# Cosine attention on one core: head 0's queries in natural order, one rsqrt chain for two heads, and the QK wave as two tasks

## The chip, the cores and the metric

The kernel runs on one core of a Trainium2 chip. The metric is the device time of one execution in microseconds (us). Runs are repeated; medians are quoted. A ratio is the mean time of one kernel's fast runs over the mean of the other's fast runs of the same rounds on the same chip, with a 95% interval, so it is not quite the ratio of the medians that are quoted.

Engine names in the profile: PE is TensorE (matmul), PEld its weight load, DVE is VectorE, ACT is ScalarE, POOL is GpSimd, SP is SyncE, which here only issues DMAs. An entry such as "SPq" or "ACTq" is such an engine issuing a DMA.

## The reference

Thirty-two heads, 2048 queries and keys each, head size 20, bfloat16. Queries and keys are normalised, the logits get one factor per head, and a softmax over the keys follows.

```python
B, H, S, D = 1, 32, 2048, 640;  Dh = D // H          # Dh = 20
def reference(q, k, v, t):
    eps = 1e-6
    qn = q / (jnp.sqrt((q * q).sum(axis=-1, keepdims=True)) + eps)
    kn = k / (jnp.sqrt((k * k).sum(axis=-1, keepdims=True)) + eps)
    logits = jnp.einsum('bhqd,bhkd->bhqk', qn, kn) * t[None, :, None, None]
    attn = _softmax(logits, axis=-1)
    return jnp.einsum('bhqk,bhkd->bhqd', attn, v)
```

## The kernel before

The program is a list of tasks. A task has an engine, a duration, its dependences and a priority. A list scheduler runs the tasks in model time and so fixes, once and for all, the order of the instructions on each engine. On the chip each engine takes its instructions in this order, and waits where a dependence isn't met (in e1 below one such wait holds VectorE for 2.5 us, with ready work behind it). **So the modelled durations and the priorities are part of the program: they decide its order.**

```python
def add(self, eng, name, fn, dur, deps=(), pri=0.0, lat=0.0, dma=None): ...

def schedule(self):                      # list scheduling in model time
    ...
    _, _, t = heapq.heappop(ready[e])    # of what is ready, the lowest pri first
    t.start = now
    t.end = now + t.dur
    if e == "PE":
        kind = t.name[:2]
        if kind != last_pe[0]:
            t.end += 0.09                # modelled cost of a change of kind, qk or pv
    ...
    order[e].append(t)
```

The exponentials of the logits are shared between two engines. A unit is 128 keys by 512 queries. Most units go to ScalarE in **waves** of three: TensorE computes QK for three units into one of two PSUM slots, ScalarE takes one exponential of 128x1536 from PSUM into a ring of 36 units in SBUF, and TensorE later multiplies four units of the ring with V (PV). The rest goes to VectorE in **tiles** of four units, which get an approximate exponential by integer arithmetic: four evictions of 128x512 from the single PSUM bank `psD`, then three operations on 128x2048 integers and one multiplication. A tile gives TensorE four QK matmuls and three PV groups. A head has 16 rows of four units; 3 or 4 of the rows are VectorE tiles.

```python
DVE_TILES = [4 if h % 3 == 1 else 3 for h in range(H)]          # 107 tiles in all
...
def add_wave(w):
    us = waves[w]; slot = w % 2
    def f_qk(eng, tk):      # first two units that use different halves of the PE rows
        pair = next(((i, i + 1) for i in range(len(us) - 1)
                     if A_units[us[i]][2] // 2 != A_units[us[i + 1]][2] // 2), ())
        for i in list(pair) + [i for i in range(len(us)) if i not in pair]:
            h, r, g = A_units[us[i]]
            last = qk_mm(eng, h, r, g, psA[...], 32 if w < WPLAIN else 64 if i in pair else 128)
        return last
    deps = [act.get(w - 2)] + ...
    qk = add("PE", f"qkA{w}", f_qk, 0.24 if w < WPLAIN else 0.55 if len(us) > 1 else 0.24,
             deps, due_a(us[0]) - 100)
    ...
    act[w] = add("ACT", f"exp{w}", ..., 0.065 + n / 1200.0, [qk] + war, 0)
```

In front of this stands the **preparation** of a head: load, square, sum, an inverse square root by a bit trick and two Newton steps (eight small operations that depend on each other), normalise, transpose by DMA, rotate the keys by DMA.

```python
def add_prep(h):
    due = h - 2.2                          # priority of this head's preparation
    for nh in range(4):                    # queries, permuted: four strided loads
        src = bass.AP(q.tensor, q[0, h].offset + nh * D, [[16 * D, 32], [4 * D, 4], [512 * D, 4], [1, D]])
        ...                                # ldq on SP (two of head 0's on ACT)
    ...                                    # ldk, ldv on SP; ldv waits only for its buffer
    dv("sq", ...128x640..., 0.86); dv("sum", ..., 0.86)
    dv("rs", ...128x32..., 0.12)           # eight of these, one after the other
    norm[h] = dv("norm", ...128x640..., 0.86)
    trn[h] = ...; rot[h] = ...             # DMA transpose, rotated copies
```

Of the kernel before, what the change touches and what calls it, by code (L numbers as in the profile page):

```python
# [12 lines left out]
I32 = mybir.dt.int32  # L13
# [26 lines left out]
class Program:  # L40
# [75 lines left out]
    def plan_waits(self, sem_of):  # L116
# [55 lines left out]
def bass_standalone__qk_norm__prompt_kernel(  # L172
# [13 lines left out]
    NB = 4  # L186
    NT = 3
    NX = 3
    DVE_TILES = [4 if h % 3 == 1 else 3 for h in range(H)]
    WPLAIN = 5  # L190
    PE_GROUP = 0.23
    SH_ENG, SH_DUR = "DVE", 0.60

    with ExitStack() as es:  # L194
# [6 lines left out]
        vaug = [sbuf(f"vaug{i}", [128, R, 32], BF16) for i in range(NB)]  # L201
        sq = sbuf("sq", [128, 2 * R, D], F32)
        rs = {x: sbuf(f"rs_{x}", [128, 2 * R], F32) for x in ("sum", "u", "a", "b", "y", "r")}
        qkn = [sbuf(f"qkn{i}", [128, 2 * R, 32], BF16) for i in range(2)]
# [5 lines left out]
        xt = [sbuf(f"xt{i}", [128, 2048], I16) for i in range(NX)]  # L210
        ee = [sbuf(f"ee{i}", [128, 2048], I16) for i in range(NX)]
        ss = [sbuf(f"ss{i}", [128, 2048], I16) for i in range(NX)]
        mm = [sbuf(f"mm{i}", [128, 2048], I16) for i in range(2)]
        tt = [sbuf(f"tt{i}", [128, 2048], FP16) for i in range(NX)]
# [10 lines left out]


        def memset(ap, val):
            return lambda eng, tk: eng.memset(ap, val)

        ld_t = add("SP", "ld_t", lambda eng, tk: eng.dma_start(  # L230
            tb16[:, :], bass.AP(t.tensor, 0, [[0, 128], [1, H]])), 0.06, lat=2.5, dma="t", pri=-50)
        scr0 = add("DVE", "scr0", memset(act_scr[:, :], 0.0), 0.1, pri=-100)
        warm = add("ACT", "warm", lambda eng, tk: eng.activation(
            act_scr[:, :], act_scr[:, :], ACT.Exp), 1.5, [scr0], pri=-100)
        z_qkn = [add("POOL", "z", memset(qkn[i][:, :, D:32], 0.0), 0.5, pri=-90 + i) for i in range(2)]
        z_qz = [add("DVE" if i else "POOL", "z", memset(qz[i][:, :, :], 0.0), 1.8, pri=-85 + i) for i in range(NT)]
        z_kx = add("POOL", "z", memset(kx[:, :], 0.0), 0.9, pri=-95)
        z_v = []
        for i in range(NB):
            a = add("POOL", "z", memset(vaug[i][:, :, D + 1:32], 0.0), 0.3, pri=-80 + i)  # L240
            b = add("POOL", "z", memset(vaug[i][:, :, D:D + 1], 1.0), 0.2, pri=-80 + i)
            z_v.append([a, b])
        tcp = add("DVE", "tcp", lambda eng, tk: eng.tensor_copy(t_f32[:, :], tb16[:, :]), 0.1, [ld_t], pri=-1)
# [3 lines left out]
        for h in range(H):  # L247
            nd = DVE_TILES[h]
            for r in range(R - nd):

                A_units += [(h, (g + r) % 4 if h == 0 and r < 4 else r, g) for g in range(NG)]
            D_tiles += [(h, r) for r in range(R - nd, R)]
        NA = len(A_units)
        nA_head = [(R - DVE_TILES[h]) * NG for h in range(H)]
        a0 = [sum(nA_head[:h]) for h in range(H + 1)]
        waves = [list(range(i, min(i + WAVE, NA))) for i in range(0, NA, WAVE)]

# [5 lines left out]
        ld_v, norm, trn, rot = {}, {}, {}, {}  # L263
        qk_users = {h: [] for h in range(H)}
        pv_users = {h: [] for h in range(H)}

# [3 lines left out]
        prep_deps = []  # L270
        qz0 = []

        def add_prep(h):
            b, b2, bt = h % NB, h % 2, h % NT
            due = h - 2.2
            war = ([norm[h - NB]] if h >= NB else []) + ([trn[h - 2]] if h >= 2 else [])
            lds = []
            for nh in range(4):
                src = bass.AP(q.tensor, q[0, h].offset + nh * D,
                              [[16 * D, 32], [4 * D, 4], [512 * D, 4], [1, D]])  # L280
                dst = qk_sb[b][32 * nh:32 * nh + 32, 0:R, :].rearrange("p (c g) d -> p c g d", g=4)
                lds.append(add("ACT" if h == 0 and nh >= 2 else "SP", f"ldq{h}", lambda eng, tk, dst=dst, src=src: eng.dma_start(dst, src),  # L282
                               0.6, war, due - 0.5 + 0.01 * (nh >= 2), lat=2.5, dma=f"q{b}a" if h == 0 and nh >= 2 else f"q{b}"))
            src_k = k[0, h].rearrange("(p r) d -> p r d", p=128)
            lds.append(add("SP", f"ldk{h}", lambda eng, tk: eng.dma_start(qk_sb[b][:, R:2 * R, :], src_k),
                           0.6, war, due - 0.51, lat=2.5, dma=f"k{b}"))
            src_v = v[0, h].rearrange("(p r) d -> p r d", p=128)
            warv = pv_users[h - NB] if h >= NB else z_v[b]
            ld_v[h] = add("SP", f"ldv{h}", lambda eng, tk: eng.dma_start(vaug[b][:, :, 0:D], src_v),
                          0.6, warv, due - 0.4, lat=3.0, dma=f"v{b}")  # L290

            def dv(name, fn, dur, deps):
                return add("DVE", name + str(h), fn, dur, deps, due)
            x = qk_sb[b]
            c = [dv("sq", lambda eng, tk: eng.tensor_tensor(sq[:, :, :], x[:, :, :], x[:, :, :], ALU.mult),  # L295
                    0.86, lds + prep_deps)]
            c.append(dv("sum", lambda eng, tk: eng.tensor_reduce(rs["sum"][:, :], sq[:, :, :], AXIS_X, ALU.add),  # L297
                        0.86, [c[-1]]))
            c.append(dv("rs", lambda eng, tk: eng.tensor_scalar(
                rs["u"][:, :].bitcast(I32), rs["sum"][:, :].bitcast(I32), -0.5, 1597463007.0, ALU.mult, ALU.add),  # L300
                0.12, [c[-1]]))
            cur = rs["u"]
            for tgt in (rs["y"], rs["r"]):
                c.append(dv("rs", lambda eng, tk, cur=cur: eng.tensor_tensor(  # L304
                    rs["a"][:, :], cur[:, :], cur[:, :], ALU.mult), 0.12, [c[-1]]))
                c.append(dv("rs", lambda eng, tk: eng.scalar_tensor_tensor(  # L306
                    rs["b"][:, :], rs["a"][:, :], -0.5, rs["sum"][:, :], ALU.mult, ALU.mult), 0.12, [c[-1]]))
                c.append(dv("rs", lambda eng, tk, cur=cur, tgt=tgt: eng.scalar_tensor_tensor(
                    tgt[:, :], rs["b"][:, :], 1.5, cur[:, :], ALU.add, ALU.mult), 0.12, [c[-1]]))
                cur = tgt  # L310
            c.append(dv("rs", lambda eng, tk: eng.tensor_scalar(
                rs["r"][:, 0:R], rs["r"][:, 0:R], t_f32[:, h:h + 1], None, ALU.mult), 0.12, [c[-1], tcp]))
            if h == 0:
                first_head(x, c[-1])
                return
            war = [trn[h - 2]] if h >= 2 else [z_qkn[b2]]
            norm[h] = dv("norm", lambda eng, tk: eng.tensor_tensor(  # L317
                qkn[b2][:, :, 0:D], x[:, :, :], bc(rs["r"][:, :], 2 * R), ALU.mult), 0.86, [c[-1]] + war)
            prep_deps[:] = [norm[h]]

            war = (qk_users[h - NT] + [*rot[h - NT]] + (qz0 if h == NT else [])) if h >= NT else []
            trn[h] = add("SP", f"trn{h}", lambda eng, tk: eng.dma_start_transpose(
                qkT[bt][:, :].rearrange("p (c n) -> p c n", n=128),
                qkn[b2][:, :, :].rearrange("p r d -> p (r d)")), 0.1, [norm[h]] + war, due + 0.1,
                lat=3.0, dma=f"T{bt}")
            rot[h] = []
            for g in range(NG):
                rot[h].append(add("SP", f"qz{h}", lambda eng, tk, g=g: eng.dma_start(
                    qz[bt][32 * g:32 * g + 32, g, :], qkT[bt][32 * g:32 * g + 32, 0:512]), 0.6,
                    [trn[h], z_qz[bt]], due + 0.15, lat=2.0, dma=f"Z{bt}"))  # L330
            for dl in range(1, 4):
                n = 128 - 32 * dl
                for (d0, s0, m) in ((0, 32 * dl, n), (n, 0, 32 * dl)):
                    rot[h].append(add("SP", f"rot{h}", lambda eng, tk, d0=d0, s0=s0, m=m, dl=dl: eng.dma_start(
                        kR[bt][d0:d0 + m, dl - 1, :], qkT[bt][s0:s0 + m, 512:1024]), 0.6, [trn[h]], due + 0.2,
                        lat=2.0, dma=f"R{bt}"))

        def first_head(x, rinv):
            kv = kx[:, :].rearrange("p (e c g w) -> p e c g w", e=4, c=4, g=4)
            src = x[:, R:2 * R, :]  # L340
            nk = add("DVE", "normk0", lambda eng, tk: eng.tensor_tensor(
# [37 lines left out]

        first_pv = {}  # L380

        def pv_mm(eng, h, lhsT, rhs_of):
            start = h not in first_pv
            first_pv[h] = True
            last = None
# [185 lines left out]
```

## Time and profile before

| | before |
|---|---|
| median | 752.0 us |
| span of the profiled run | 750.1 us |
| exponentials on ScalarE | 540 |
| first exponential starts | 16.49 us |
| last one ends, then the tail | 745.57 us, 4.5 us |

The first view is the page's table of engines: busy time, share of the span, instructions. Below it is the chain of waits: the work that ended last, followed back step by step, as shares of the span by engine.

```profile
PE 697.3 (93%) x4952; PEld 191.7 (26%) x4952; DVE 724.1 (97%) x1315; ACT 727.6 (97%) x542; POOL 5.5 (1%) x16
...
ACT 95%; PE 2%; DVE 1%; DMA 1%; SPq 0%; ACTq 0%; issue 0%; DVEq 0%
```

The next view is ScalarE's timeline. The columns are start and length in us, engine and line, operation, destination and source, shapes and count; in brackets stands the idle time before the row and what ended it. Rows without a gap are merged.

```profile
16.49 1.45 ACT L438 ACTIVATE p_ring<-psA 128x1536 bf16<-128x1536 f32 x1 [13.46 <-PE psA L378]
19.11 5.62 ACT L438 ACTIVATE p_ring<-psA 128x1536 bf16<-128x1536 f32 x4 [1.17 <-PE psA L378]
25.43 1.45 ACT L438 ACTIVATE p_ring<-psA 128x1536 bf16<-128x1536 f32 x1 [0.70 <-PE psA L378]
27.92 717.65 ACT L438 ACTIVATE p_ring<-psA 128x1536 bf16<-128x1536 f32 x534 [1.03 <-PE psA L378]
```

Two readings. ScalarE is the limit: from 27.92 us on, 534 exponentials take 717.65 us, 1.344 us each, without a visible gap. And the start costs 16.49 us, with three more gaps after it (1.17 + 0.70 + 1.03 = 2.90 us). VectorE and TensorE are over 90% busy as well.

### The profile page before, as it was taken

The numbers are of one execution on the slowest core, as the hardware profiler recorded it, in microseconds if no ns is written. First come the engines' busy times: TensorE is split into PE (matmuls) and PEld (weight loads), VectorE is DVE, ScalarE is ACT, GpSimd is POOL, SyncE is SP. The second block draws the span as 40 slices with busy tenths as digits, with TensorE's granted clock in tenths as the row PEclk, the third lists the DMA queues.
The fourth block names the chain that finished last, engine by engine and source line by source line (L and its number), as shares of the span: only waits on it lengthen the run. The fifth ranks groups of instructions, "written<-read, shape, count | busy, mean of one in ns | idle before, by whom it ended". The sixth has DMA issues, their size and how long they took to land.

```text
span 750.1 us, 12494 instructions
## 1 busy us (share of the span) xinstructions
PE 697.3 (93%) x4952; PEld 191.7 (26%) x4952; DVE 724.1 (97%) x1315; ACT 727.6 (97%) x542; POOL 5.5 (1%) x16
## 2 busy tenths in 40 slices
PE   0999999999999999999999999999999999999997
PEld 0222222222222222222222222222222222222221
DVE  6799999999999999999999999999999999999997
ACT  1899999999999999999999999999999999999997
POOL 2000000000000000000000000000000000000000
PEclk9999999999999999999999999999999999999999
DMA  6323332233223333232322233323223232321200
GB/s 74 64 51 61 62 58 43 32 54 61 54 44 49 49 48 59 54 51 39 55 46 56 46 53 53 49 46 61 55 36 49 47 56 52 59 33 30 47 6 5
DMA packets 199466, 36.49 MB, mean 49 GB/s; under 512 B 175216, under 2 KB 199408, under 8 KB 199408
## 3 DMA queue, kind: packets, MB, share of 16 engines
q1 hardware_dynamic: 198352, 35.66, 29.5%
q8 instruction: 39, 0.64, 0.4%
q10 hardware_dynamic: 1056, 0.04, 0.1%
q14 instruction: 19, 0.16, 0.1%
HBM read 7.87 MB, written 2.62 MB: 14 GB/s over the span
## 4 chain that ended last, share of the span: by engine, by line
ACT 95%; PE 2%; DVE 1%; DMA 1%; SPq 0%; ACTq 0%; issue 0%; DVEq 0%
ACT p_ring L438 95%; PE psA L378 1%; DMA kR<-kx 1%; PE psO L387 1%; PE psD L378 0%; DMA qk_sb<-in_q_dram 0%; DVE rs_sum L297 0%; DVE sq L295 0%; ACTq L194 0%; DVE kx L349 0%; DVE rs_b L306 0%; DVE rs_a L304 0%; SPq L282 0%; DVE oT L396 0%; DVE xt L466 0%
## 5 line engine op out<-in xcount | busy, mean ns | idle before, releaser
L438 ACT ACTIVATE p_ring<-psA 128x1536 bf16<-128x1536 f32 x540 | 726.1, 1608 | 16.4 <-PE psA L378 16.4
L378 PE MATMUL psA<-qz,kR 64*128 64x512 bf16 (+1 forms) x1204 | 318.6, 389 | 18.0 <-ACT p_ring L438 13.3
L466 DVE TENSOR_SCALAR xt<-psD 128x512 int16<-128x512 f32 x428 | 292.8, 684 | 19.0 <-PE psD L378 15.4
L387 PE MATMUL psO<-p_ring,vaug 128*32 128x512 bf16 x1620 | 155.4, 388 | 1.0 <-ACT p_ring L438 0.9
L378 PEld LDWEIGHTS psA<-qz,kR 64*128 64x128 bf16 (+1 forms) x1204 | 83.3, 94 | 233.9 <-ACT p_ring L438 127.0
L378 PE MATMUL psA<-qz,qkT 64*128 64x512 bf16 (+1 forms) x401 | 131.7, 389 | 6.0 <-ACT p_ring L438 4.3
L479 DVE TENSOR_TENSOR tt<-xt,mm 128x2048 f16<-128x2048 f16 x107 | 130.2, 1217 | 0.1
L378 PE MATMUL psD<-qz,kR 128*128 128x512 bf16 x318 | 122.5, 385 | 2.4 <-DVE xt L466 1.1
L471 DVE TENSOR_SCALAR ee<-xt 128x2048 int16<-128x2048 int16 x107 | 73.4, 686 | 0.2
L474 DVE TENSOR_SCALAR ss<-xt 128x2048 int16<-128x2048 int16 x107 | 73.3, 685 | 0.0
L476 DVE TENSOR_SCALAR mm<-xt 128x2048 int16<-128x2048 int16 x107 | 73.3, 685 | 0.0
L387 PEld LDWEIGHTS psO<-p_ring,vaug 128*32 128x32 bf16 x1620 | 39.3, 94 | 85.7 <-issue 73.7
L378 PEld LDWEIGHTS psA<-qz,qkT 64*128 64x128 bf16 (+1 forms) x401 | 31.9, 94 | 76.0 <-ACT p_ring L438 40.5
L378 PEld LDWEIGHTS psD<-qz,kR 128*128 128x128 bf16 x318 | 30.7, 97 | 53.6 <-DVE xt L466 27.2
L387 PE MATMUL psO<-ee,vaug 128*32 128x512 f16 x428 | 42.8, 390 | 1.3 <-DVE ee L471 1.2
L387 PE MATMUL psO<-tt,vaug 128*32 128x512 f16 x428 | 42.4, 386 | 1.0 <-DVE tt L479 0.4
L387 PE MATMUL psO<-ss,vaug 128*32 128x512 f16 x428 | 42.5, 387 | 0.1
L378 PE MATMUL psD<-qz,qkT 128*128 128x512 bf16 x106 | 41.0, 386 | 0.8 <-DVE xt L466 0.5
L295 DVE TENSOR_TENSOR sq<-qk_sb 128x640 f32<-128x640 bf16 x32 | 26.1, 816 | 0.3 <-DMA qk_sb<-in_q_dram 0.3
L297 DVE TENSOR_REDUCE rs_sum<-sq 128x32 f32<-128x640 f32 x32 | 25.9, 810 | 0.1
L317 DVE TENSOR_TENSOR qkn<-qk_sb,rs_r 128x640 bf16<-128x640 bf16 x31 | 25.3, 815 | 0.1
L396 DVE STREAM_TRANSPOSE oT<-psO 128x512 f32<-128x512 f32 x32 | 22.7, 710 | 1.5 <-PE psO L387 1.4
(37 smaller groups left out, 134.3 us busy)
## 6 DMA issues: line engine op xcount, KB each, us to landing
kR<-qkT SPq DMA_DIRECT2D x62, 96.0 KB, 2.1
qz<-qkT SPq DMA_DIRECT2D x128, 32.0 KB, 1.9
kR<-qkT SPq DMA_DIRECT2D x62, 64.0 KB, 2.0
qk_sb<-in_k_dram SPq DMA_DIRECT2D x32, 80.0 KB, 2.1
vaug<-in_v_dram SPq DMA_DIRECT2D x32, 80.0 KB, 3.2
out_dram<-o_stage SPq DMA_DIRECT2D x32, 80.0 KB, 1.8
qk_sb<-in_q_dram SPq DMA_DIRECT2D x126, 20.0 KB, 2.5
kR<-qkT SPq DMA_DIRECT2D x62, 32.0 KB, 1.9
```

The costliest lines, as they stand in the source:

```text
L295: c = [dv("sq", lambda eng, tk: eng.tensor_tensor(sq[:, :, :], x[:, :, :], x[:, :, :], ALU.mult), 0.86, lds + prep_deps)]
L297: c.append(dv("sum", lambda eng, tk: eng.tensor_reduce(rs["sum"][:, :], sq[:, :, :], AXIS_X, ALU.add), 0.86, [c[-1]]))
L317: norm[h] = dv("norm", lambda eng, tk: eng.tensor_tensor(qkn[b2][:, :, 0:D], x[:, :, :], bc(rs["r"][:, :], 2 * R), ALU.mult), 0.86, [c[-1] ...
L378: return eng.matmul(dst, lhsT, mov, tile_position=(p0, 0))
L387: last = eng.matmul(psO[32 * g:32 * g + 32, :], lhsT(g), rhs_of(g), start=start, stop=False, skip_group_check=True, tile_position=(0, 32 * g))
L396: tr = add("DVE", f"tr{h}", lambda eng, tk: eng.transpose(oT[:, :, :].rearrange("p r d -> p (r d)"), psO[:, :]), 0.62, pv_users[h] + ([fin ...
L438: act[w] = add("ACT", f"exp{w}", lambda eng, tk: eng.activation(p_ring[:, p0 * 512:p0 * 512 + n], psA[:, slot * WAVE * 512:slot * WAVE * 5 ...
L466: t1 = add("DVE", f"t1.{j}.{g}", lambda eng, tk, g=g: eng.tensor_scalar(xt[s][:, 512 * g:512 * g + 512], psD[:, :], X_MUL, X_ADD, ALU.mult ...
L471: te = add("DVE", f"e{j}", lambda eng, tk: eng.tensor_scalar(ee[s][:, :], xt[s][:, :], 0x7C00, KE_BITS, ALU.bitwise_and, ALU.bitwise_or), ...
L474: t5 = add(SH_ENG, f"s{j}", lambda eng, tk: eng.tensor_scalar(ss[s][:, :], xt[s][:, :], float(SHIFT - 4096), None, ALU.add), SH_DUR, t1s + ...
L476: tm = add("DVE", f"m{j}", lambda eng, tk: eng.tensor_scalar(mm[s2][:, :], xt[s][:, :], 0x3FF, 0x3800, ALU.bitwise_and, ALU.bitwise_or), 0.60,
L479: tT = add("DVE", f"T{j}", lambda eng, tk: eng.tensor_tensor(tt[s][:, :], xt[s][:, :].bitcast(FP16), mm[s2][:, :].bitcast(FP16), ALU.mult) ...
```

## The change

Its intent: start ScalarE earlier, and take load off VectorE so that it can do one more tile. The parts are:

1. Head 0 loads its queries in natural order with one DMA; normalisation writes them permuted, and head 0's store undoes it with four DMAs. The value loads of later heads wait until head 0's query transpose has landed. All zero fills but a small one go to GpSimd.
2. Head 0's units that need no rotated keys come first.
3. From head 4 on, two heads share one rsqrt chain of twice the width (`NSOLO`, the heads prepared alone, is 4). Both heads get the priority of the first. The lead of a preparation over its head grows from 2.2 to 2.4 heads (`LEAD`).
4. Head 14 gets a fourth VectorE tile: 108 tiles, 1616 units, 538 full waves and one of two units.
5. A QK wave becomes two tasks, pair and single, which the scheduler's model counts as 0.23 us each, where the one task counted 0.55. The 0.09 us for a change of kind comes on top in both kernels.

The core of the diff (renames, buffer counts and the start's details are cut):

```diff
-    DVE_TILES = [4 if h % 3 == 1 else 3 for h in range(H)]
+    NSOLO = 4
+    LEAD = 2.4
+    PE_MM = 0.23
+    DVE_TILES = [4 if h % 3 == 1 or h == 14 else 3 for h in range(H)]
...
+            if h == 0:
+                A_units += [(0, 4 * c + (g + dl) % 4, g) for dl in range(4) for c in range(na // 4) for g in range(NG)]
...
-        def add_prep(h):
-            due = h - 2.2
+        def add_prep(hs):
+            due = hs[0] - LEAD
+            n = len(hs)
+            w = 2 * R * n
...
+            for i, h in enumerate(hs):          # square and sum, per head
...
-                c.append(dv("rs", ... rs["a"][:, :], cur[:, :], cur[:, :] ..., 0.12, [c[-1]]))
+                c = dv("rs", ... rs["a"][:, 0:w], cur[:, 0:w], cur[:, 0:w] ..., 0.09 + 0.03 * n, [c])
...
-            qk = add("PE", f"qkA{w}", f_qk, 0.24 if w < WPLAIN else 0.55 if len(us) > 1 else 0.24, deps, due_a(us[0]) - 100)
+            parts = [list(range(len(us)))] if plain else [x for x in (
+                pair, [i for i in range(len(us)) if i not in pair]) if x]
+            qks = [add("PE", f"qkA{w}", lambda e, tk, part=part: f_qk(e, part, 32 if plain else 64 if part is pair else 128),
+                       PE_MM * (1 if plain or part is pair else len(part)), deps, due_a(us[0]) - 100) for part in parts]
...
+        preps = [[h] for h in range(min(NSOLO, H))] + [list(range(h, min(h + 2, H))) for h in range(NSOLO, H, 2)]
```

## The prediction

> **What bounds the kernel now.** ScalarE. The list of groups has 540 exponentials (128x1536), busy 726.1 us. The chain of waits shows ScalarE alone from 32.09 us to 744.23 us: 530 exponentials in 712.14 us, 1.344 us apart, without a gap. Its waits before exponentials sum to 16.4 us, in four waits before 28 us: 13.46 before the first (it starts at 16.49), then 1.17, 0.70 and 1.03. After the last exponential come about 4.5 us. VectorE (97%) is the second limit. Time can come from fewer exponentials, an earlier start, fewer early gaps.
>
> **Removed, added, moved.**
> - Head 14 gives one more tile to VectorE: 1616 units instead of 1620, so 538 full waves and one of two units. 1.34 us plus about 0.43 us off ScalarE: -1.8 us. VectorE pays for a tile with its group durations: 4x0.684 + 3x0.686 + 1.217 = 6.0 us.
> - The rsqrt chain is eight small operations, 1.47 us busy per head. In 14 pairs of heads it runs once on twice the width; each operation grows by an estimated 0.03 us (32 more elements at the pace of the 640-element operation). Saving about 1.2 us a pair, 17 us of VectorE in all. Net VectorE busy falls to about 713 us. ScalarE bounds the steady part, so this only pays for the extra tile.
> - Start. Now the last strided query load lands at 5.25 us and the first square starts at 5.33. One natural-order query load on ScalarE's queue and the keys early on SyncE's should land by about 3.4 us: square at about 3.8. But the timeline shows the first transpose issued only at 11.25 us, though its input was ready at 9.38: SyncE was issuing four value loads, 1.17 us each. The change holds back all but one of these; instead the key and query loads of heads 1 and 2 (0.6 and 0.65 us each) stand before the transpose. I estimate its issue at 9.2 us (8.0 to 10.0), and so the first exponential at 14.4 us: -2.1 us.
> - Unrotated units first: four waves, 5.4 us of exponentials, need no rotated keys, which land about 1.9 us after the first exponential starts. The 1.17 us gap goes. The 0.70 and 1.03 us gaps come while TensorE still takes 0.60 us per matmul (later 0.39); I expect about as much to remain.
> - QK wave as two tasks: same matmuls and order of priority; it mainly changes the scheduler's model (a wave 0.46 instead of 0.55 us; the trace shows 0.64 from pair to PV). No gain; some risk of TensorE falling behind.
> - All zero fills go to GpSimd, about 10 us of them. The 1.69 us cast at 3.34 us ended with GpSimd's 1.81 us fill. That agrees with the Trainium skill, "SBUF — State Buffer", section "Who interferes with whom": cast and tensor_scalar can need a port pair that GpSimd holds for a whole instruction. The first tensor_scalar of the rsqrt chain could lose up to 1.8 us so.
>
> **Sum.** 752.0 - 1.8 - 2.1 - 1.2 = 746.9; I say 746.7 us, range 743.5 to 750.0. Faster by over 2%: 2%; within 2%: 96%; slower by over 2%: 2%.
>
> **Signs.** First exponential at 13.2 to 15.2 us; no wait over 0.3 us before the second; 539 exponentials still 1.344 us apart; ScalarE without gaps from about 30 us; VectorE busy 708 to 718 us with more idle time; 108 tiles; tail still about 4.5 us.
>
> **What would make it wrong.** ScalarE waits for TensorE in the steady part, because the schedule's cheaper wave packs too much between two waves; loads of heads 1 and 2 delay the first transpose beyond 11 us; port waits during the start.

## More of the kernel before

One more view matters later: VectorE's work on the tile `sq` (square and sum, two operations per head) in four stretches of 21 us. The columns are the stretch, its length, busy us with the count of operations, granted clock, DMA share and GB/s.

```profile
242.00:263.00 21.00, 1.63 (x2) 1.00 0.32 51
264.00:285.00 21.00, 1.63 (x2) 1.00 0.25 37
287.00:308.00 21.00, 1.62 (x2) 1.00 0.30 50
311.00:332.00 21.00, 1.63 (x2) 1.00 0.34 57
```

Every stretch holds the preparation of one head. It comes evenly.

## The result, and the profile after

The changed kernel takes 755.79 us (754.99 to 756.70, 6 runs) against 752.07 us (6 runs): ratio 1.0051, interval 1.0038 to 1.0064. A gain of 5.3 us was predicted, the result is a loss of 3.7.

The table of engines and the chain of waits of the changed kernel:

```profile
PE 702.4 (93%) x4960; PEld 194.6 (26%) x4960; DVE 719.6 (96%) x1209; ACT 731.7 (97%) x541; POOL 9.2 (1%) x24
...
ACT 59%; PE 23%; DVE 15%; DMA 1%; issue 1%; SPq 0%; DVEq 0%
```

ScalarE has one exponential fewer and yet is "busy" 4 us longer, and the chain that was ScalarE alone now goes through TensorE and VectorE for 38% of the span. Its timeline:

```profile
14.05 2.79 ACT L489 ACTIVATE p_ring<-psA 128x1536 bf16<-128x1536 f32 x2 [11.37 <-PE psA L415]
17.07 4.35 ACT L489 ACTIVATE p_ring<-psA 128x1536 bf16<-128x1536 f32 x3 [0.23 <-PE psA L415]
22.13 1.45 ACT L489 ACTIVATE p_ring<-psA 128x1536 bf16<-128x1536 f32 x1 [0.71 <-PE psA L415]
24.30 1.45 ACT L489 ACTIVATE p_ring<-psA 128x1536 bf16<-128x1536 f32 x1 [0.72 <-PE psA L415]
26.39 119.73 ACT L489 ACTIVATE p_ring<-psA 128x1536 bf16<-128x1536 f32 x88 [0.64 <-PE psA L415]
146.29 232.30 ACT L489 ACTIVATE p_ring<-psA 128x1536 bf16<-128x1536 f32 x172 [0.17 <-PE psA L415]
378.87 186.29 ACT L489 ACTIVATE p_ring<-psA 128x1536 bf16<-128x1536 f32 x137 [0.28 <-PE psA L415]
565.34 83.83 ACT L489 ACTIVATE p_ring<-psA 128x1536 bf16<-128x1536 f32 x62 [0.18 <-PE psA L415]
649.34 99.29 ACT L489 ACTIVATE p_ring<-psA 128x1536 bf16<-128x1536 f32 x73 [0.18 <-PE psA L415]
```

The start did what it should: 14.05 instead of 16.49 us, and early gaps of 0.23 + 0.71 + 0.72 + 0.64 = 2.30 us. But from 26.39 to 748.63 us ScalarE does 532 exponentials in 722.24 us, 1.358 us each instead of 1.344. **Only 0.81 us of this shows as gaps.** The rest hides: the record of an exponential is at least 1.45 us long in the steady part (mean 1.61 us before, 1.52 after) and begins while the one before still runs, so one that is up to 0.1 us late (1.45 - 1.343) leaves no gap. It shows in the pitch (the time from one end to the next) and in the chain, not in the idle column. The difference of the two spans (753.2 - 750.1 = 3.1 us) is the sum of these terms:

| term | us |
|---|---|
| first exponential earlier | -2.44 |
| early gaps | -0.60 |
| 538 exponentials and a short one instead of 540 | -1.7 |
| **late exponentials after the early gaps** | **+7.8** |
| tail (4.59 instead of 4.52) | +0.1 |

Below, "small stalls" is the sum, from the 14th exponential on, of what the pitch exceeds 1.343 us (its median in every run), read from the single records, for excesses under 0.45 us; larger ones are named singly. Before: 0.35 us. After: 8.0 us, no large one, 78 of them over 0.025 us.

TensorE's timeline in one place where two waves in three are late, in the changed kernel:

```profile
280.88 0.39 PE L415 MATMUL psA<-qz,kR 64*128 64x512 bf16 x2
281.21 0.39 PE L415 MATMUL psA<-qz,qkT 128*128 128x512 bf16 x1
281.53 0.40 PE L424 MATMUL psO<-p_ring,vaug 128*32 128x512 bf16 x4
281.75 0.39 PE L424 MATMUL psO<-tt,vaug 128*32 128x512 f16 x4
282.07 0.39 PE L415 MATMUL psA<-qz,kR 64*128 64x512 bf16 x2
282.39 0.39 PE L415 MATMUL psA<-qz,qkT 128*128 128x512 bf16 x1
282.62 0.38 PE L415 MATMUL psD<-qz,kR 128*128 128x512 bf16 x1
282.93 0.40 PE L424 MATMUL psO<-p_ring,vaug 128*32 128x512 bf16 x4
283.16 0.39 PE L424 MATMUL psO<-ee,vaug 128*32 128x512 f16 x4
283.48 0.39 PE L415 MATMUL psA<-qz,kR 64*128 64x512 bf16 x2
```

TensorE never waits here. A wave with two other groups takes 282.07 - 280.88 = 1.19 us, one with three takes 283.48 - 282.07 = 1.41 us, and ScalarE needs a wave every 1.343. So three other groups in wave after wave are too many. (The kernel before also has waves of three, 173 of them to 174 after. But the longest run of waves with three or more is 3 before and 9 after.) The pair takes 0.32 us to the single, which takes another 0.32 to a PV group: 0.64 us. The model counts 0.46 and 0.09 for the change of kind from PV to QK, 0.55 in all. What it misses is the second change, from pair to single: 0.09 us per wave. The old 0.55 allowed for it.

The other places are alike. Before 65 of the 78 late exponentials (6.9 of their 7.7 us) TensorE hardly waited: in the 1.5 us up to the start of their last QK group, its groups exceeded the median pitch for their shapes by less than 0.1 us in sum.

What changed on VectorE: the same view of `sq` as above, in the changed kernel.

```profile
242.00:263.00 21.00, 3.25 (x4) 1.00 0.26 26
264.00:285.00 21.00, 0.00 (x0) 1.00 0.41 77
287.00:308.00 21.00, 3.21 (x4) 1.00 0.14 12
311.00:332.00 21.00, 0.00 (x0) 1.00 0.43 77
```

And the tile `tt` of the changed kernel in the same stretches; the columns after the length are PE, PEld and DVE, each busy us with its count.

```profile
242.00:263.00 21.00, 0.80 (x8) 0.20 (x8) 2.43 (x2) 1.00 0.26 26
264.00:285.00 21.00, 1.59 (x16) 0.41 (x16) 4.83 (x4) 1.00 0.41 77
287.00:308.00 21.00, 0.96 (x12) 0.20 (x8) 2.43 (x2) 1.00 0.14 12
311.00:332.00 21.00, 1.59 (x16) 0.41 (x16) 5.50 (x5) 1.00 0.43 77
```

Two heads are prepared together, then none for a whole head's time. VectorE's count on `tt` is one per finished tile: 2, 4, 2, 5 to the stretch. In the single records, 14 stretches longer than 10 us, from the start of one operation of the preparation to the start of the next, hold none of them; they last 22 to 27 us. (Before there is one of 12.4 us.) In them TensorE gets 0.76 PV groups from tiles per exponential, elsewhere 0.47. Up to the last preparation, 66 exponentials from the 14th on are over 0.025 us late; 43 of them start 15 to 40 us after the start of the latest operation of the preparation.

### The profile page after: what moved, and what is told of

It is laid out like the page before. It is cut to its first block, busy times and chain, and to the rows that moved or that the text cites. A ratio compares the mean times of both kernels' runs of the same rounds, so it can differ in the third digit from the quotient of the medians.

```text
span 753.2 us, 12434 instructions
## 1 busy us (share of the span) xinstructions
PE 702.4 (93%) x4960; PEld 194.6 (26%) x4960; DVE 719.6 (96%) x1209; ACT 731.7 (97%) x541; POOL 9.2 (1%) x24
## 4 chain that ended last, share of the span: by engine, by line
ACT 59%; PE 23%; DVE 15%; DMA 1%; issue 1%; SPq 0%; DVEq 0%
ACT p_ring L489 59%; PE psA L415 11%; PE psO L424 8%; DVE xt L522 6%; PE psD L415 5%; DVE tt L536 4%; DVE mm L534 1%; DVE ee L530 1%; DVE ss L532 1%; DVE sq L320 1%; DVE rs_sum L322 1%; DMA kR<-kx 1%; SPq L234 0%; DVE qkn L348 0%; DMA qk_sb<-in_k_dram 0%
## 5 line engine op out<-in xcount | busy, mean ns | idle before, releaser
L424 PE MATMUL psO<-p_ring,vaug 128*32 128x512 bf16 x1616 | 152.1, 388 | 0.6 <-DVE oT L436 0.4
L415 PE MATMUL psA<-qz,qkT 64*128 64x512 bf16 (+1 forms) x392 | 128.6, 388 | 4.0 <-ACT p_ring L489 3.2
```

Source lines behind the costliest of these rows:

```text
L415: return eng.matmul(dst, lhsT, mov, tile_position=(p0, 0))
L424: last = eng.matmul(psO[32 * g:32 * g + 32, :], vaug[h % NV][:, r_of(g), :], rhs_of(g), start=start, stop=False, skip_group_check=True, ti ...
```

## The experiments

Theories at the start. **M**: the model counts a wave too cheaply, so the fixed order crowds TensorE. **T**: splitting a wave into two tasks costs by itself. **V**: preparing two heads together makes bursts. **X**, added later: the extra tile does it. Each run was timed in 5 rounds; its median is over its 4 or 5 runs (6 for the changed kernel). The kernel before took 751.6 to 752.1 us beside all of them. The 95% intervals reach at most 0.0017 to either side of the ratio, so e7 and e8 can't be told from the kernel before.

| run | wave counts | chain | tiles | us | ratio to before | small stalls, us |
|---|---|---|---|---|---|---|
| changed kernel | 2 x 0.23 | two heads | 108 | 755.79 | 1.0051 | 8.0 |
| e1 | 0.55 | two heads | 108 | 759.80 | 1.0107 | 1.7, and five large: 8.5 |
| e2 | 2 x 0.275 | two heads | 108 | 760.69 | 1.0117 | 2.2, and six large: 9.0 |
| e3 | 0.46 | two heads | 108 | 755.76 | 1.0045 | 7.8 |
| e4, the kernel before | 0.46 | one head | 107 | 753.77 | 1.0022 | 2.0 |
| e5 | 2 x 0.275 | two heads | 107 | 754.45 | 1.0035 | 2.5, and two large: 1.6 |
| e6 | 2 x 0.23 | two heads | 107 | 755.24 | 1.0048 | 5.5 |
| e7 | 2 x 0.275 | one head | 107 | 751.67 | 0.9997 | 0.4 |
| e8 | 2 x 0.23 | one head | 107 | 751.52 | 0.9998 | 2.8 |
| e9 | 2 x 0.23 | one head, in bursts | 107 | 756.86 | 1.0071 | 8.0 |
| e10 | 2 x 0.275 | one head | 107, other heads | 749.88 | 0.9980 | 1.4 |
| e11 | 2 x 0.23 | two heads, spread | 107 | 759.68 | 1.0098 | 5.2, and four large: 4.1 |
| e12 | 2 x 0.275 | one head, old unit order | 107 | 754.81 | 1.0040 | 0.8 |
| e13 | 2 x 0.23 | one head | 108 | 763.42 | 1.0148 | 8.7, and one large: 1.6 |

### e1, e2, e3: the wave's modelled cost, and the split

e1 puts the wave back to one task of 0.55, e2 keeps two tasks that sum to 0.55, e3 takes one task of 0.46.

```diff
 # e1 (e3: 0.46)
-            qks = [add(... one per part ..., PE_MM * (1 if plain or part is pair else len(part)), ...)]
+            def f_all(e, tk):
+                for part in parts:
+                    last = f_qk(e, part, 32 if plain else 64 if part is pair else 128)
+                return last
+            qks = [add("PE", f"qkA{w}", f_all, PE_MM if plain or len(us) == 1 else 0.55, deps, due_a(us[0]) - 100)]
 # e2
-                       PE_MM * (1 if plain or part is pair else len(part)), ...
+                       PE_MM if plain else 0.275, ...
```

> The changed kernel with the QK wave put back to one task that the scheduler's model counts as 0.55 us (instead of two of 0.23). Theory M (the model counts a wave too cheaply, so the fixed order packs more TensorE work between two waves than fits in 1.343 us): about 749 us (747.5 to 751), ScalarE's excess over 1.343 us per exponential from us 30 on falls from about 7 us to below 1.5 us. Theory T (splitting the wave in two tasks costs by itself): also about 749. Theory V (preparing two heads together makes VectorE's work, and so TensorE's, come in bursts): stays at 755 to 756.

> The changed kernel, two tasks kept, each counted as 0.275 us by the scheduler's model, so a wave counts 0.55. Theory M: about 749 us, as e1. Theory T: stays at 755 to 756. Theory V: stays at 755 to 756.

> The changed kernel with one task per wave, counted as 0.46 us like the two tasks together. Theory M: stays at 755 to 756 with about 7 us of excess. Theory T: about 749. Theory V: stays at 755 to 756.

e3 equals the changed kernel and e2 nearly equals e1, so **T falls**: the split does nothing, only the number does. M is half right. With 0.55 the small stalls fall from 8.0 to about 2 us, close to M's 1.5, but the time went up by 4 us instead of down by 7. ScalarE's timeline of e1, four rows of it, shows why:

```profile
26.99 346.43 ACT L492 ACTIVATE p_ring<-psA 128x1536 bf16<-128x1536 f32 x257 [0.72 <-PE psA L415]
375.13 44.52 ACT L492 ACTIVATE p_ring<-psA 128x1536 bf16<-128x1536 f32 x33 [1.71 <-PE psO L424]
422.71 147.87 ACT L492 ACTIVATE p_ring<-psA 128x1536 bf16<-128x1536 f32 x110 [3.06 <-PE psO L424]
572.65 1.45 ACT L492 ACTIVATE p_ring<-psA 128x1536 bf16<-128x1536 f32 x1 [2.07 <-PE psA L415]
```

Two of the new large stalls wait for PV (`psO`), that is, for free places in the ring. They come after head 14, where heads 13, 14 and 16 now have four tiles. The program's own model time, in which it fixes the order, can be read: with 0.55 it has exactly these two stalls, 1.4 us before exponential 264 and 3.0 us before 297 (the chip's are 1.8 and 3.2), and none when the extra tile is taken back. So they are the schedule's choice, not the chip's surprise. The third, at 572 us, is not in the model, but e1's trace shows it. VectorE's order has `sq` of the next pair at 570.09 us, and this waited 2.46 us for its query load, which SyncE issued only from 565.4 to 568.1 us, after the rotation copies of the pair before. The eviction of `psD` behind it came at 570.84, and TensorE, whose next QK needs `psD`, waited 2.73 us, with the QK wave behind that. Then TensorE's granted clock stood at 0.50 of full speed from 573.1 to 576.5 us, with matmul records of 0.61 us instead of 0.39, and the last two large stalls (574 and 576 us) fall there. e2's stalls at 572 and 661 us and all four of e11's show the same: `sq` waits for its query load. e5's two are of the kind as well, as the load landed 0.08 us before `sq` started. No run with one head at a time has such a stall. The tail also grew, from 4.6 to 6.3 us.

### e4: the cheap number in the kernel before

```diff
-            qk = add("PE", f"qkA{w}", f_qk, 0.24 if w < WPLAIN else 0.55 if len(us) > 1 else 0.24, ...
+            qk = add("PE", f"qkA{w}", f_qk, 0.24 if w < WPLAIN else 0.46 if len(us) > 1 else 0.24, ...
```

> The kernel before with one number changed: the model counts a wave as 0.46 us instead of 0.55. Theory M: slower than before by 3 to 7 us (755 to 759), with gaps or pitches over 1.343 us on ScalarE spread over the run. Theories T and V: 752, unchanged.

One number makes the kernel before 1.8 us slower, with 2.0 us of small stalls. The direction is M's, the size misses its range: M alone does not make 8 us.

### e5 to e8: pairing, the number and the extra tile apart

e5 is e2 without the extra tile, e6 the changed kernel without it. e7 and e8 are the same two with one-head chains.

```diff
-    DVE_TILES = [4 if h % 3 == 1 or h == 14 else 3 for h in range(H)]
+    DVE_TILES = [4 if h % 3 == 1 or False else 3 for h in range(H)]      # e5, e6, e7, e8
-                       PE_MM * (1 if plain or part is pair else len(part)), ...
+                       PE_MM if plain else 0.2750, ...                   # e5, e7
-    NSOLO = 4
+    NSOLO = 32                                                            # e7, e8
```

> The changed kernel with two numbers changed: a wave counted as 0.55 us by the scheduler's model, and no extra VectorE tile in head 14 (107 tiles, 540 exponentials). Theory M+X (the cheap wave makes the scattered small stalls of ScalarE, the extra tile makes the large ones that e1 and e2 showed at 377, 424 and 574 us): 749 to 752 us, small stalls below 2.5 us in all, none over 0.45 us. Rival R (the paired preparation or the new lead time makes the steady part slow whatever the model counts): 755 us or more, large stalls still there.

> The changed kernel with only the extra tile of head 14 taken back (wave still counted as 0.46). Theory M: small stalls stay at 6 to 8 us, time 756 to 758.5 (one exponential and a third more than the changed kernel, 1.8 us). Rival X alone (the extra tile is what makes TensorE's work burst): small stalls below 2.5 us, 749 to 752.

> As e5, with the rsqrt chain of one head at a time (about 17 us more of VectorE's time). If pairing is worth nothing in the steady part, as predicted, because ScalarE bounds it: within 0.7 us of e5. If VectorE's saved time matters there: slower than e5 by 2 us or more. If pairing makes bursts (theory V): faster than e5.

> As e6 (wave counted as 0.46, 107 tiles), with the rsqrt chain of one head at a time. Theory V (with pairing, VectorE's tiles and so TensorE's work come in bursts, which is why the cheap wave costs about 7 us in the changed kernel but only 1.7 us in the kernel before, e4): small stalls fall to about 2 us, 750 to 752.5. Theory M alone: small stalls stay at 6 to 8 us as in e6, 756 to 758.5.

e5 missed both expectations: 754.45 lies between them. e6 gave 5.5 us of small stalls, just below M's range, and 755.24 us, faster than M said. What decides is e7 against e5 and e8 against e6. **Undoing the pairing gains 2.8 and 3.7 us**, at either number (e5 to e7, e6 to e8), although the new lead stays, and although VectorE is then busy 8 us longer (724.1 against 716.2 in e7 and e5; 722.3 against 715.0 in e8 and e6). Small stalls fall from 2.5 to 0.4, and from 5.5 to 2.8. That speaks for V. Between e7 and e8 the number moves 2.4 us of stalls, but e7 gives it back in its tail (6.6 us against 4.1, because with 0.55 VectorE is the last to finish).

### e9: the bursts alone

If bursts do it, they must hurt without the two-head chain. e9 is e8 with one line changed; each head keeps its own chain, and VectorE keeps all its work.

```diff
-            due = hs[0] - LEAD
+            due = (hs[0] - hs[0] % 2 if hs[0] >= 4 else hs[0]) - LEAD
```

> As e8 (one-head rsqrt chains, wave counted 0.46, 107 tiles), with one number changed: the odd head of each pair gets the priority of the even one, so two heads are again prepared back to back, without the two-head chain and without its saving of VectorE time. Theory V (what hurts is that the preparation comes in bursts and leaves VectorE long stretches of tile work only, which asks more of TensorE than it can do beside ScalarE's waves): small stalls of ScalarE rise from 2.8 us (e8) to 4 to 6 us (e6 had 5.5), time 753.5 to 756. Rival W (the two-head chain itself, its width or the VectorE time that it saves, is what hurts): stalls stay at 2 to 3 us, 751 to 752.5.

756.86 us (ratio 1.0071, e8 0.9998), small stalls 8.0 us: more than V expected, and far from W's range. VectorE's work on `sq` in two neighbouring stretches of e9, the same view as above:

```profile
254.00:275.00 21.00, 1.63 (x2) 1.00 0.18 40
277.00:297.00 20.00, 0.00 (x0) 1.00 0.47 64
```

The single records again show 14 stretches over 10 us without preparation, now 13 to 25 us long. Of 7.7 us of lateness (exponentials over 0.025 us late), 6.0 us lie in waves before which six waves in a row saw no operation of the preparation (e8: 0.4 of 2.4 us). The longest run of waves with three or more other groups is 8 (e8: 4), and before 59 of the 62 late exponentials TensorE hardly waited, by the measure above. A priority reorders everything, so the tail could have moved too, but it is 4.4 us against e8's 4.1: the loss is in the small stalls. So **the bursts cost by themselves**, at least with the wave counted as 0.46; neither the width of the chain nor the time that it saves is needed for the loss.

### e10: a version that beats both

```diff
 # on e7
-    DVE_TILES = [4 if h % 3 == 1 or False else 3 for h in range(H)]
+    DVE_TILES = [4 if h % 3 == 0 else 3 for h in range(H)]
```

> The candidate for the best version: as e7 (changed start, one-head chains, wave counted 0.55, 107 tiles) with the four-tile heads at 0, 3, ... 30 instead of 1, 4, ... 31, so that the last head has three tiles and VectorE is not the last to finish. In e7 ScalarE was done at 743.25 us and 6.6 us followed; expected here: ScalarE done at 743 to 745, a tail of 4 to 5 us, 748.5 to 750.5 us. If the tail of e7 is not due to the last head's fourth tile: 751.5 as e7.

749.88 us, ratio 0.9980 (0.9968 to 0.9993) to the kernel before: a small gain, but clear of noise. The tail fell from e7's 6.6 to 4.6 us, as expected. This is e7's start, with one head prepared at a time:

```profile
14.04 2.79 ACT L489 ACTIVATE p_ring<-psA 128x1536 bf16<-128x1536 f32 x2 [11.34 <-PE psA L415]
...
24.28 718.87 ACT L489 ACTIVATE p_ring<-psA 128x1536 bf16<-128x1536 f32 x534 [0.72 <-PE psA L415]
```

From 24.28 us on there is no gap, and 1.346 us per exponential.

### e11: pairing, but spread

```diff
 # on e6: square and sum one head earlier for the first head, normalisation one later for the second
-                return add("DVE", name + str(hs[0]), fn, dur, deps, due)
+                return add("DVE", name + str(hs[0]), fn, dur, deps, due + off)   # off = i - n + 1, or i
```

> As e6 (two-head chain, wave counted 0.46, 107 tiles), with the per-head parts of the preparation given the priority of their own head (squares and sums one head earlier for the first, normalisation one head later for the second). Theory V: small stalls fall from 5.5 us (e6) to 3 to 4.5 us, as the spreading is only partial; rival W: they stay at 5 to 6 us.

This failed: 759.68 us (the profiled run took 757.78), with four large stalls. Small stalls 5.2 us are within W's range and not V's. A priority only orders what is ready, and the records still show 21 stretches over 10 us without preparation. So the edit did not spread the work, and the run decides nothing between V and W.

### e12: the unit order of head 0

```diff
 # on e7
-                A_units += [(0, 4 * c + (g + dl) % 4, g) for dl in range(4) for c in range(na // 4) for g in range(NG)]
-                rest = range(na // 4 * 4, na)
+                A_units += [(0, (g + r) % 4 if r < 4 else r, g) for r in range(na) for g in range(NG)]
+                rest = []
```

> As e7, with the unit order of the kernel before in head 0 (rotated units from the second wave on). If the unrotated units first are what took the 1.17 us gap away: the second exponential again waits over 1 us for the rotated keys, and the time rises by about 1 us over e7 (752.3 to 753). If the early gaps only come later instead: same time as e7 within 0.4 us.

The gap before the second exponential is back, 1.14 us. The last exponential ends 1.5 us later than in e7 (744.78 against 743.25); 0.5 us of this is a later first exponential, which varies between runs with this same start (14.04 to 14.30 us in some, 14.59 or 14.60 in others). The time rose by more, 3.1 us, because the tail went from 6.6 to 8.9 us: the other order moved everything behind it.

### e13: only the pairing undone in the changed kernel

```diff
-    NSOLO = 4
+    NSOLO = 32
```

> The changed kernel with the rsqrt chain of one head at a time and nothing else changed (108 tiles, wave counted 0.46). Theory V (bursts of preparation are the largest single cost): small stalls of ScalarE fall from 8 us to 3 to 4.5 us, the 15 to 30 us stretches of tile work vanish, time 751 to 753.5. If the saved VectorE time is needed for the 108th tile: large stalls (over 0.45 us) of 1 to 3 us appear around the heads after 14, and the time stays at 753.5 to 756.

Both expectations missed by far: 763.42 us, small stalls of 8.7 us, a tail of 10.3 us. The chain of waits:

```profile
DVE 39%; PE 29%; ACT 28%; issue 2%; DMA 1%; SPq 0%
```

VectorE leads it, and it is also the last engine to finish. **With 108 tiles the pairing is needed; without it the 108th tile costs 11.9 us (763.42 against e8's 751.52).** So the parts can't be priced one at a time. The extra tile needs VectorE time that only the pairing gives, and the pairing brings the bursts. Together they cost 4.3 us (755.79 against e8's 751.52), for 1.7 us fewer exponentials. Why the 108th tile, an estimated 5.3 us of VectorE (four evictions and three operations at a pitch of 0.6 us, one at 1.13), costs so much more than its own length is open in part. About half of it is in the fixed order: in the program's own model time e13 ends 5.5 us later than e8, with a tail of 8.7 us where e8 has 2.7, and its one large stall stands there with 1.2 us (the chip's is 1.6). On the chip the granted clock also stood at 0.50 from 753.9 us on.

## Why the prediction was wrong

The failed step is the sentence "ScalarE bounds the steady part, so this only pays for the extra tile", with its sign "exponentials still 1.344 us apart; ScalarE without gaps from about 30 us". I priced pairing and extra tile by the amount of work on each engine. All three compute engines were over 90% busy, held together by a fixed order, and the change altered when VectorE does its work. Late exponentials cost 7.8 us, where the sum had zero; bursts alone cost 5.3 us in time where a run isolated them (e9 against e8). The extra tile, which the saving was to pay for, gained nothing (e6 without it took 755.24 us, the changed kernel 755.79).

- **The start: right.** First transpose issued at 9.51 us (predicted 9.2), first square at 3.98 (3.8), first exponential at 14.05 (14.4). Part of this was luck. The issue came 1.74 us earlier; the other 0.70 us came because it lasted 1.32 us instead of 2.02, which I had not foreseen, so that the query transpose behind it came 2.44 us earlier. These rows show SyncE issuing the transposes of head 0, two rows before and three after:

```profile
11.25 2.02 SPq L351 DMA_TRANSPOSE qkT<-kx  x1
13.32 1.25 SPq L354 DMA_TRANSPOSE qkT<-qkn  x1
...
9.51 1.32 SPq L389 DMA_TRANSPOSE qkT<-kx  x1
10.88 1.25 SPq L392 DMA_TRANSPOSE qkT<-qkn  x1
12.18 1.51 SPq L395 DMA_TRANSPOSE kR<-kx  x1
```

- **Unrotated units first: right.** The 1.17 us gap is gone; e12 brought 1.14 us back. The gaps in the slow-matmul time stayed, as predicted.
- **Fewer exponentials: right** (1.7 us; 1.8 predicted). The tail too: 4.59 us, 4.5 predicted.
- **VectorE's saving: mis-sized.** I took 0.18 us per chain operation and got 17 us. Undoing the pairing shows 7 to 8 us with 107 tiles and 9.9 us with 108 (e13 against the changed kernel), and VectorE was busy 719.6 us, not 708 to 718. In VectorE's timeline of the changed kernel an operation of the chain is followed after 0.13 us:

```profile
256.47 0.22 DVE L330 TENSOR_TENSOR rs_a<-rs_y 128x64 f32<-128x64 f32 x1
256.60 1.22 DVE L536 TENSOR_TENSOR tt<-xt,mm 128x2048 f16<-128x2048 f16 x1
```

  The Trainium skill, "Perfetto Trace Analysis", section "Optimizing Scalar/DVE Operations", says this: an overhead of about 60 ns of busy time per VectorE instruction on SBUF, and a profiled latency about twice that, as the second half overlaps with the next instruction. An estimate from that page's figure: pairing saves one such overhead in each of eight operations of 14 pairs, 14 x 8 x 0.06 = 6.7 us. The records give the pitch itself where another operation follows: 0.099 us single (e8), 0.132 paired (e6), medians, so an estimate of 14 x 8 x (2 x 0.099 - 0.132) = 7.4 us. The runs agree with the page, and I should have used the pitch and not the record.
- **The split wave: right that it does nothing by itself** (e3), and the named risk, "the schedule's cheaper wave packs too much between two waves", came true in the small stalls. Measured alone it is 1.8 us in the kernel before (e4); without pairing it moved stalls but no time (e7, e8).
- **The bursts: not foreseen.** At 107 tiles they are the largest cost that a single edit isolated: e9 against e8 is 5.2 us of small stalls, from one priority. That the mechanism is TensorE overload in the long tile-only stretches is read from the groups per exponential, the runs of full waves and the late exponentials before which TensorE hardly waited; no run changed TensorE's load alone, so that part is read from traces, not shown by an experiment. Pairing has a second cost, the late query loads: 1.6 us in e5, none over 0.45 us in the changed kernel.
- **GpSimd's port: as cited.** The cast now took 0.29 instead of 1.69 us. But the six small key copies on VectorE, which now fall into GpSimd's 1.8 us fills (6.12 to 9.68 us), took 2.08 us instead of 0.90. That agrees with the Trainium skill, "SBUF — State Buffer", section "Who interferes with whom". It stayed off the path of the first exponential; the second use, the first rsqrt operation, lost only 0.07 us (0.25 against 0.18); that was luck, as the fill beside it ended at 5.91 us, 0.22 us after the operation's start.

Open: the rest of e13's loss, and why the six times of the changed kernel fall into two groups, 755.0 to 755.2 and 756.4 to 756.7.

## What to carry to other kernels

When several engines are nearly full and a fixed order ties them together, judge a change by when the work arrives, not only by how much there is: batching two preparations saved VectorE 7 to 8 us, yet the version with one at a time was faster. Check the limiting engine by the pitch of its operations, since overlapping records hide lateness that no idle column shows. And treat the durations in a scheduling model as code: 0.09 us in one of them moved the time by 1.8 us.

## What the Trainium skill lacked or had wrong

- "TensorEngine Tiling (Array Packing)", section "Key Properties", says that a change of tiling mode drains TensorE, but gives no figure. Here the next group starts 0.226 us after one of the same shape and 0.31 to 0.33 us after one of another (pair to single 0.322, single to PV 0.320, medians), so a change costs about 0.09 us. A wave has two of them and takes 0.64 us; the changed model counts one of them, 0.55.
- "TensorE: Matmul & The Clock Gate", section "What's actually happening", gives a warm-up of about 3.4 us of sustained work. Here matmul records stayed at 0.60 us or more from 13.39 to about 25.3 us in the changed kernel, with waits in between of up to 1.6 us. That is no contradiction, as the work was not sustained, and the page warns that the warm-up varies between runs; it lacks how much waiting still counts as sustained.
- "Perfetto Trace Analysis", section "Optimization Strategy", tells the reader to find the gaps between slices on the engine that limits. Here 7.8 us of ScalarE's time went with 0.81 us of visible gaps after the start. For ScalarE no page that I read says to compare the pitch.
